# Sparse attention and token mixing on one core: first-pair edge units without decoding, first queries loaded earlier, half of the second pair's keys loaded later

## The chip, the core and the metric

The kernel runs on one NeuronCore of a Trainium2 chip. Its engines are named as in the profile: PE (TensorE) does matmuls, PEld is PE's weight load, DVE (VectorE) and ACT (ScalarE) do elementwise work and reductions, POOL (GpSimd) copies and issues indirect loads, and SP (SyncE) issues the other DMA transfers, one after the other, in program order. All transfers share 16 DMA engines. The metric is the device time of one execution in microseconds (us).

## The reference, cut to what matters

Block-sparse attention over 4 batches of 8 heads, 768 positions of 64 elements, in blocks of 32 (24 blocks). A query block attends to its neighbours, to the first and the last block, and to three sampled blocks; the first and the last query block attend to everything. The result, 512 wide, goes through token mixing.

```python
def _attn_ref(q, k, v, sampled_blocks):
    ...
    scores = scale * np.matmul(q, k.transpose(0, 1, 3, 2))
    ...
    mask = np.abs(blk_i - blk_j) <= window
    mask = mask | (blk_i == 0) | (blk_j == 0) | (blk_i == n_blocks - 1) | (blk_j == n_blocks - 1)
    for qb in range(n_blocks):
        for kb in sampled_blocks[qb]:
            mask[qb * block:(qb + 1) * block, kb * block:(kb + 1) * block] = True
    ...
    attn = attn / (np.sum(attn, axis=-1, keepdims=True) + 1e-09)
    return np.matmul(attn, v)

def _moe_ref(x, w_theta, w_tok_r, w_tok_i, w_ch):
    theta = x @ w_theta
    zr, zi = x * np.cos(theta), x * np.sin(theta)
    y = np.einsum('ts,bsd->btd', w_tok_r, zr) + np.einsum('ts,bsd->btd', w_tok_i, zi)
    u = x + y
    return u + np.maximum(u @ w_ch, 0.0)
```

## The kernel before

**Pairs and units.** The four batches are worked on as two pairs (`bp` 0 and 1). Each pair has 26 units: four wide or edge units, `WIDE`, which are the first and last query blocks for a quarter of the heads at a time (`b`, `pp`), against all keys; then 22 middle units, one for each query block from 1 to 22. So units 0 to 3 are the first pair's edge units, 4 to 25 its middle units, 26 to 29 and 30 to 51 those of the second pair.

**One unit.** PE computes scores (`S`, line 314; `SW`, line 407, for edge units), DVE takes a minimum of the negated scores (lines 316 and 413), ACT the exponential (lines 325 and 421), PE transposes the weights (`T` and `Tw`, line 331) into one PSUM tile, ACT copies that to `pT` (line 333), and PE multiplies with the values (`X`, line 365, once for two middle units; `Xw`, line 435). DVE divides by the sums (`xo`, line 350), and SP stores the result in DRAM (`xs`, lines 384 and 446).

**What a unit needs.** Middle units read keys that POOL gathers from the pair's key tile into `kg` (`gather_k`, line 275), since the sampled blocks are known only at run time; POOL then issues an indirect load of values, `vb` (line 297), and SP loads the neighbours' values, `va` (lines 293 and 294). Edge units read the key tile itself: it has eight groups, four for each `b`, and the unit (`b`, `pp`) reads groups 4b + pp·2 and the next. They read values that `load_v_wide` loads (780 KB each, line 397). Queries are loaded for two blocks at once (256 KB, line 236) and scaled by ACT (line 242).

**Keys.** The first pair's key tile lies in a room that later becomes weights and, before that, the second pair's values for edge units; the second pair's key tile `kb1` is a room of its own, loaded one group (384 KB) at a time, in eight loads (line 250), during units 5 to 19.

**Decoding.** The mixing weights arrive as 64-bit floats and are turned into a high and a low 32-bit part during attention, piece by piece. A piece has three phases: ACT takes the absolute value (line 69) and DVE rearranges bits (73 to 75); DVE scales the low word (81 and 83); ACT rounds to the high part (line 89) and DVE takes the rest (96 and 97). When a piece is done, SP loads the next but one (line 64). 20 pieces, 60 phases, are shared out over the units by weight: 1.5 for an edge unit, 1 for a middle unit, 0 for some. `decoder.ahead` issues ACT's part and `decoder.go` DVE's.

**Order.** The order is written out by hand in a loop over units `n`; each engine runs its instructions in that order. Loop `n` issues the scores of unit n + 1, the transposes and values of unit n (or of a pair of units before), and the gathers and scaling for unit n + 2. On ACT, `scale_q` of unit n + 2 comes first in a loop, ahead of unit n's `pT` copy, and `decoder.ahead` stands between the first `pT` copy of an edge unit and the next unit's exponential. Key and value loads for the second pair are SP instructions at the head of a loop; stores and `va` loads come at its end.

Of the kernel before, what the change touches and what calls it, by code (L numbers as in the profile page):

```python
# [193 lines left out]
def attention(tc, qT, qE, kT, vr, sampled, xs, ident, pieces, room, follow):  # L194
# [9 lines left out]
    with ExitStack() as ctx, ExitStack() as scored, ExitStack() as early:  # L204
# [27 lines left out]
        def load_q(bp, i):  # L232
            if i % 2 == 0:
                return
            t = qp.tile([P, 2, 2, 4, 32], F32, tag="q", name=f"q{bp}_{i}", bufs=Q_BUFS)
            nc.sync.dma_start(t.rearrange("r u b p f -> r u (b p f)"), qT[bp][:, i - 1 : i + 1, :])
            qbs[bp, i] = t
# [10 lines left out]
        def load_k(bp, g, n, s=slice(0, NB)):  # L248
            b = g // 4
            nc.sync.dma_start(kbs[bp][:, g : g + n, s], kT[bp, b][:, g - 4 * b : g - 4 * b + n, s])  # L250
# [5 lines left out]
        def load_edges(bp):  # L256
            qes[bp] = ep.tile([P, 2, 4, 64], F32, tag="qe", name=f"qe{bp}")
            nc.sync.dma_start(qes[bp].rearrange("r b p f -> r (b p f)"), qE[bp])

        def turn_edges(bp):  # L260
            t = qes[bp].rearrange("r b p f -> r (b p f)")
            nc.vector.tensor_scalar(t, t, -0.125, None, op0=ALU.mult)
# [125 lines left out]
        def load_v_wide(bp, b, pp):  # L388
            k = 2 * b + pp - 1
            if k < 0:  # L390
                v = vp.tile([P, 6, 260], F32, tag="vw", name=f"vw{bp}")
            else:
                if not k:
                    vrooms[bp] = room(("tok_r", "tok_i")[bp], f"vw{bp}").rearrange("p c f -> p (c f)")
                v = vrooms[bp][:, 1560 * k : 1560 * k + 1560].rearrange("p (c f) -> p c f", f=260)
            c0 = 260 * (2 * b + pp)
            nc.sync.dma_start(v, vr[768 * bp : 768 * bp + 768, c0 : c0 + 260].rearrange("(c s) f -> s c f", s=P))
            vws[bp, b, pp] = v
# [49 lines left out]
        WIDE = [(b, pp) for b in range(2) for pp in range(2)]  # L448
        units = []
# [1 line left out]
            units += [(bp, "w", x) for x in WIDE] + [(bp, i, None) for i in range(1, NB - 1)]  # L451
        shares, total = [], 0.0
        for n in range(len(units)):
            if n < 2 or n >= len(units) - 2 or units[n][1:] == ("w", WIDE[-1]):
                weight = 0.0
            else:
                weight = 1.5 if units[n][1] == "w" else 1.0
            total += weight
            shares.append(total)

        def do(n, inner, wide=None):

            if 0 <= n < len(units):
                bp, i, x = units[n]
                if i != "w":
                    inner(bp, i)
                elif wide:
                    wide(bp, *x)
# [4 lines left out]
        def first_of_pair(n):  # L473
            return n < len(units) and units[n][1] == "w" and units[n][2] == (0, 0)
# [3 lines left out]
        with tc.manual_schedule():  # L478
            load_edges(0)
            load_k(0, 0, 2, slice(0, 16))  # L480
            load_k(0, 0, 2, slice(16, NB))
            turn_edges(0)
            load_k(0, 2, 2)
            tab = Tables(nc, wp, sampled)
            load_v_wide(0, 0, 0)
            load_k(0, 4, 2)
            load_v_wide(0, 0, 1)
            load_k(0, 6, 2)
            load_v_wide(0, 1, 0)
            load_v_wide(0, 1, 1)  # L490
            for i in (1, 3):
                load_q(0, i)
            decoder = Decoder(pieces, stage, nc.sync)
            idle = ps_t.tile([P, 8, 128], F32, tag="T", name="idle")

            def turn_idle(n):
                for k in range(n):
                    nc.tensor.transpose(idle[:, k % 8, :], ident, ident)

            turn_idle(16)  # L500
            do(0, scores, scores_wide)
            turn_idle(10)
            tab.make(nc, cp)
            do(0, weights, weights_wide)
            for n in range(len(units) + 1):
                phases = 0
                if n < len(units):
                    phases = round(shares[n] / total * 3 * len(pieces)) - decoder.at
                if n + 5 < len(units) and not is_wide(n + 5) and units[n + 5][:2] not in ((0, 1), (0, 3)):
                    load_q(*units[n + 5][:2])  # L510
                if first_of_pair(n + 10):
                    load_edges(1)
                if first_of_pair(n + 12):
                    load_v_wide(1, 0, 0)
                for before, x in zip((2, 1, 0), WIDE[1:]):
                    if n and first_of_pair(n + before):
                        load_v_wide(1, *x)
                do(n + 2, gather_k)
                if n == len(units) - 16:
                    follow.send(vp)  # L520
                elif len(units) - 16 < n < len(units) - 4:
                    next(follow)
                elif n == len(units) - 3:
                    next(follow)
                if 5 <= n < 21 and n % 2:
                    load_k(1, (n - 5) // 2, 1)
                do(n + 3, number_blocks)
                do(n + 2, scale_q)
                if first_of_pair(n + 2):
                    turn_edges(1)  # L530
                if not is_wide(n):
                    decoder.ahead(phases)
                last = None
                if is_wide(n):
                    bp, _, x = units[n]
                    if n and not is_wide(n - 1):
                        last = units[n - 2][:2]
                        values(*last)
                        finish(*last)
                    turn_wide(bp, *x, 0)  # L540
                    decoder.ahead(phases)
                    do(n + 1, scores, scores_wide)
                    if n and is_wide(n - 1):
                        values_wide(bp, *units[n - 1][2], 1)
                    if is_wide(n + 1):
                        nx = units[n + 1]
                        weights_wide(nx[0], *nx[2], (0,))
                        turn_wide(bp, *x, 1)
                        weights_wide(nx[0], *nx[2], (1,))
                    else:  # L550
                        turn_wide(bp, *x, 1)
                        do(n + 1, weights, weights_wide)
                    values_wide(bp, *x, 0)
                    if n and is_wide(n - 1):
                        finish_wide(bp, *units[n - 1][2])
                    decoder.go(phases)
                    if n == 0:
                        tab.rest(nc)
                elif n == len(units):
                    last = units[n - 2][:2]  # L560
                    values(*last)
                    next(follow)
                    finish(*last)
                else:
                    bp, i, _ = units[n]
                    do(n + 1, scores, scores_wide)
                    if n == len(units) - 2:
                        early.close()
                        next(follow)
                    if i == 1:  # L570
                        values_wide(bp, *units[n - 1][2], 1)
                    elif i % 2:
                        last = bp, i - 2
                        values(*last)
                    if n == len(units) - 1:
                        scored.close()
                        next(follow)
                    if i % 2 and i > 1:
                        do(n + 1, weights, weights_wide)
                        if n == len(units) - 2:  # L580
                            next(follow)
                        turn(bp, i)
                    else:
                        turn(bp, i)
                        do(n + 1, weights, weights_wide)
                    decoder.go(phases)
                    if last:
                        finish(*last)
                    if n == len(units) - 1:
                        next(follow)  # L590
                    if i == 1:
                        finish_wide(bp, *units[n - 1][2])
                do(n + 2, load_pair)
                do(n + 2, gather_v)
            assert not decoder.left(), decoder.left()
            ctx.close()
            next(follow)
# [363 lines left out]
```

## Time and profile before

| | us |
|---|---|
| median of three runs | 586.22 |
| lowest and highest | 585.17, 587.04 |
| the profiled execution | 584.9 |
| its span, first to last instruction | 583.1 |
| PE busy in the span | 544.0 |
| DVE busy | 438.9 |
| ACT busy | 344.7 |
| POOL busy | 147.9 |

The profiled execution has 1.8 us around its span. Attention reaches from the start to about 233 us, where POOL ends, and token mixing from there to the end. The profile's timelines give, for one engine, start and length of each group of like instructions, its line in the kernel, the operation, what it writes and reads, and, in brackets, how long the engine stood idle before it and what released it. "issue" there means that the engine waited for nothing that the profile shows.

### The profile page before, as it was taken

To read this page: it belongs to the slowest core of one execution; us is meant where nothing else is said; L and a number is where in the kernel's file an instruction comes from. 1 tells how busy PE (TensorE), PEld (TensorE's weight loads), DVE (VectorE), ACT (ScalarE), POOL (GpSimd) and SP (SyncE) were. 2 spreads that over 40 slices of the span, in tenths; PEclk is the share of its full clock that TensorE was granted. 3 is DMA by queue.
4 is the path that set the end of the run, shared out by engine and by line. 5 is a ranking of instruction groups with operands and counts; after the bars stand their busy time and mean duration, and the time that the engine had idled before them with its cause. 6 is when DMAs were issued, how large, how long until landed. Compare 5 with 4: busy or idle time off the path is not lost.

```text
span 583.1 us, 16870 instructions
## 1 busy us (share of the span) xinstructions
PE 544.0 (93%) x6662; PEld 481.6 (83%) x6662; DVE 438.9 (75%) x1011; ACT 344.7 (59%) x734; POOL 147.9 (25%) x262
## 2 busy tenths in 40 slices
PE   7798888799989888999899999999999999999997
PEld 5465655566656666899899999999999999999997
DVE  4576888787889898879999896749848559547454
ACT  3685866767888777856766553456434456434510
POOL 1457768642589885000000000000000000000000
PEclk9998988999999989999999999999999999999999
DMA  8979899977699997545233333212421111212002
GB/s 293 351 216 323 260 364 349 300 241 271 200 299 291 317 296 227 156 123 151 85 100 101 105 115 98 65 44 61 136 84 63 57 48 46 78 55 72 6 1 108
DMA packets 64975, 95.60 MB, mean 164 GB/s; under 512 B 9216, under 2 KB 46976, under 8 KB 64896
## 3 DMA queue, kind: packets, MB, share of 16 engines
q1 hardware_dynamic: 58560, 71.09, 40.1%
q0 software_dynamic: 6336, 23.43, 12.1%
q8 instruction: 52, 0.85, 0.6%
q14 instruction: 27, 0.22, 0.1%
HBM read 81.90 MB, written 12.58 MB: 162 GB/s over the span
## 4 chain that ended last, share of the span: by engine, by line
PE 73%; DVE 8%; ACT 8%; issue 4%; SPq 3%; DMA 3%; ACTq 0%; DVEq 0%
PE y L721 10%; PE y L723 10%; PE y L722 10%; PE X L365 7%; PE T L331 6%; PE S L314 4%; PE o L744 4%; PE o L745 4%; PE o L746 4%; PE h L670 3%; PE h L669 3%; PE h L671 3%; ACT pT L333 3%; ACT P L325 2%; DMA q<-in_qT_dram 2%
## 5 line engine op out<-in xcount | busy, mean ns | idle before, releaser
L325 ACT ACTIVATE P<-S,m 128x256 f32<-128x256 f32 x176 | 69.3, 486 | 7.7 <-DVE m L316 7.3
L333 ACT COPY pT<-T 128x1024 f32<-128x1024 f32 x44 | 44.9, 1021 | 32.8 <-PE T L331 32.6
L316 DVE TENSOR_REDUCE m<-S 128x4 f32<-128x1024 f32 x44 | 53.6, 1218 | 13.8 <-PE S L314 13.5
L331 PE MATMUL T<-ident,P 128*128 128x128 f32 x352 | 51.7, 289 | 10.1 <-ACT pT L333 6.4
L331 PEld LDWEIGHTS T<-ident,P 128*128 128x128 f32 x352 | 39.9, 146 | 22.9 <-ACT pT L333 15.0
L676 ACT ACTIVATE t<-h,up_int 128x256 f32<-128x256 f32 x48 | 22.7, 475 | 58.6 <-PE h L671 55.6
L275 POOL COPY kg<-kb 128x256 f32 (+2 forms) x101 | 52.9, 564 | 17.1 <-PE S L314 17.0
L275 POOL COPY kg<-kb_tok_i 128x256 f32 (+2 forms) x101 | 48.4, 519 | 24.3 <-DMA kb_tok_i<-in_kT_dram 14.5
L297 POOL DMA_INDIRECT vb<-in_vr_dram,rows x44 | 44.6, 1013 | 38.8 <-PE X L365 33.6
L671 PE MATMUL h<-w_theta_hi,xTl 128*128 128x256 f32 x192 | 54.1, 282 | 0.2 <-DVE xTl L661 0.2
L669 PE MATMUL h<-w_theta_hi,xTh 128*128 128x256 f32 x192 | 54.1, 282 | 0.0
L314 PE MATMUL S<-kg,q 64*32 64x256 f32 x1408 | 51.5, 387 | 2.5 <-issue 2.4
L670 PE MATMUL h<-w_theta_lo,xTh 128*128 128x256 f32 x192 | 53.9, 281 | 0.0
L721 PE MATMUL y<-w_tok_r,zh 128*128 128x384 f32 x128 | 43.2, 337 | 0.8 <-ACT zh L701 0.8
L722 PE MATMUL y<-w_tok_i,zh 128*128 128x384 f32 x128 | 43.1, 337 | 0.0
L722 PE MATMUL y<-w_tok_r,zh 128*128 128x384 f32 x128 | 43.1, 336 | 0.0
L745 PE MATMUL o<-ul,w_ch_hi 128*128 128x384 f32 x128 | 42.9, 335 | 0.0
L746 PE MATMUL o<-uh,w_ch_lo 128*128 128x384 f32 x128 | 42.9, 335 | 0.0
L721 PE MATMUL y<-w_tok_i,zh 128*128 128x384 f32 x128 | 42.8, 337 | 0.0
L744 PE MATMUL o<-uh,w_ch_hi 128*128 128x384 f32 x128 | 42.4, 335 | 0.0
L723 PE MATMUL y<-w_tok_r,zl 128*128 128x384 f32 x128 | 42.4, 336 | 0.0
L686 ACT ACTIVATE cs<-rr 128x256 f32<-128x256 f32 x48 | 20.0, 416 | 37.9 <-DVE rr L681 37.6
(157 smaller groups left out, 1438.8 us busy)
## 6 DMA issues: line engine op xcount, KB each, us to landing
xa<-xs SPq DMA_DIRECT2D x192, 64.0 KB
out_dram<-of SPq DMA_DIRECT2D x32, 192.0 KB
va<-in_vr_dram SPq DMA_DIRECT2D x22, 260.0 KB
q<-in_qT_dram SPq DMA_DIRECT2D x22, 256.0 KB
xs<-xo SPq DMA_DIRECT2D x88, 64.0 KB
xr<-xs SPq DMA_DIRECT2D x84, 64.0 KB
raw_tok_r<-in_w_tok_r_dram SPq DMA_DIRECT2D x8, 512.0 KB
raw_tok_i<-in_w_tok_i_dram SPq DMA_DIRECT2D x8, 512.0 KB
```

The costliest lines, as they stand in the source:

```text
L275: nc.gpsimd.tensor_copy(dst, blocks.rearrange("r g s f -> r s g f"))
L314: nc.tensor.matmul(sc[32 * p : 32 * p + 32, e, b, :], q[rows, b, p, :], keys[rows, :, :, place(b, p), :], start=True, stop=True)
L325: nc.scalar.activation(pt[:, e, b, :], sc[:, e, b, :], AF.Exp, bias=m[:, e, b : b + 1], scale=-1.0)
L331: nc.tensor.transpose(t[:, k, :], pt, ident)
L669: nc.tensor.matmul(ps, hi[:, c, :], wh[:, c, :], start=c == 0, stop=False)
L670: nc.tensor.matmul(ps, hi[:, c, :], wl[:, c, :], start=False, stop=False)
L671: nc.tensor.matmul(ps, lo[:, c, :], wh[:, c, :], start=False, stop=c == 3)
L721: nc.tensor.matmul(acc, zh[:, dd], wh[j][:, tt], start=j == 0 and m == 0, stop=False)
L722: nc.tensor.matmul(acc, zh[:, dd], wl[j][:, tt], start=False, stop=False)
L723: nc.tensor.matmul(acc, zl[:, dd], wh[j][:, tt], start=False, stop=j == 5 and m == 1)
L745: nc.tensor.matmul(ps, wh[:, c, :], ul, start=False, stop=False)
L746: nc.tensor.matmul(ps, wl[:, c, :], uh, start=False, stop=c == 3)
```

## The change

Four edits to the written-out order; the bytes loaded are the same, in six key loads instead of eight.

1. Units 0 to 3 get no share of the decoding (before: units 0, 1 and 3 got none, unit 2 had weight 1.5). All later shares grow a little, as the 60 phases are now spread over a weight of 46.5 instead of 48.
2. The load of the first two query blocks goes to SP ahead of the last edge unit's value load instead of behind it.
3. The second pair's three later value loads for edge units each move one loop back: from loops 24, 25 and 26 to 25, 26 and 27.
4. Of the second pair's keys, groups 0 to 3 are loaded one at a time in loops 5, 9, 13 and 17, groups 4 and 5 together in loop 24, groups 6 and 7 together in loop 25 (before: one group in each odd loop from 5 to 19).

```diff
         for n in range(len(units)):
-            if n < 2 or n >= len(units) - 2 or units[n][1:] == ("w", WIDE[-1]):
+            if n < len(WIDE) or n >= len(units) - 2 or units[n][1:] == ("w", WIDE[-1]):
                 weight = 0.0
             else:
                 weight = 1.5 if units[n][1] == "w" else 1.0
...
             load_v_wide(0, 1, 0)
+            load_q(0, 1)
             load_v_wide(0, 1, 1)
-            for i in (1, 3):
-                load_q(0, i)
+            load_q(0, 3)
             decoder = Decoder(pieces, stage, nc.sync)
...
                 if first_of_pair(n + 12):
                     load_v_wide(1, 0, 0)
-                for before, x in zip((2, 1, 0), WIDE[1:]):
-                    if n and first_of_pair(n + before):
+                for before, x in zip((1, 0, -1), WIDE[1:]):
+                    if n > 1 and first_of_pair(n + before):
                         load_v_wide(1, *x)
                 do(n + 2, gather_k)
...
-                if 5 <= n < 21 and n % 2:
-                    load_k(1, (n - 5) // 2, 1)
+                if n in (5, 9, 13, 17):
+                    load_k(1, (n - 5) // 4, 1)
+                for before, g in ((2, 4), (1, 6)):
+                    if n and first_of_pair(n + before):
+                        load_k(1, g, 2)
                 do(n + 3, number_blocks)
```

## The prediction

> **What bounds the kernel now.** I read the page first for the span, then three stretches of the span side by side, then the timelines of the start, and last the PE timeline where the chain of waits says "issue".
>
> ```profile
> span 583.1 us, 16870 instructions
> ```
>
> ```profile
> 45.00:117.00 72.00, 59.50 (x1401) 42.70 (x1402) 57.79 (x85) 50.30 (x101) 52.85 (x90) 0.93 0.99 323
> 117.00:147.00 30.00, 27.69 (x522) 18.79 (x525) 24.20 (x42) 21.99 (x33) 9.09 (x15) 1.00 0.76 243
> 233.00:583.00 350.00, 342.88 (x2237) 340.29 (x2231) 254.53 (x702) 177.59 (x423) 0.00 (x0) 1.00 0.28 82
> ```
>
> The columns are the stretch and its length, then busy time (and instructions) of PE, PE's weight loads, DVE, ACT and POOL, the granted clock, the DMA share and GB/s. The last 350 us are token mixing, with PE busy for 342.88 of them: a microsecond saved ahead of 233 us comes out at the end as one. The change lies ahead of it, in attention. There no compute engine is full. From 45 to 117 us (middle units of the first pair) PE works 59.50 of 72 us, and the DMA engines are at a share of 0.99 with 323 GB/s: transfers are what is full, and half the change takes bytes out of this stretch. From 117 to 147 us (the second pair's edge units, where those bytes go) the share is 0.76.
>
> The start is read from the timelines of ACT, DVE, PE, POOL and SP.
>
> ```profile
> 23.79 0.63 ACT L242 ACTIVATE q<-q 128x512 f32<-128x512 f32 x1 [2.44 <-DMA q<-in_qT_dram]
> 24.32 0.78 ACT L333 COPY pT<-Tw 128x768 f32<-128x768 f32 x1
> 26.37 0.68 ACT L69 ACTIVATE da_theta<-raw_theta 128x512 f32<-128x512 f32 x1 [1.27 <-DMA raw_theta<-in_w_theta_dram]
> 26.95 0.90 ACT L421 ACTIVATE PW<-SW,mw 128x768 f32<-128x768 f32 x1
> 27.73 0.80 ACT L333 COPY pT<-Tw 128x768 f32<-128x768 f32 x1
> ...
> 23.04 1.82 DVE L413 TENSOR_REDUCE mw<-SW 128x1 f32<-128x768 f32 x2 [3.32 <-PE SW L407]
> ...
> 22.85 0.92 PE L435 MATMUL Xw<-vw_tok_r,pT 128*64 128x65 f32 x24
> 25.16 0.87 PE L331 MATMUL Tw<-ident,PW 128*128 128x128 f32 x6 [1.39 <-ACT pT L333]
> 28.59 0.87 PE L331 MATMUL Tw<-ident,PW 128*128 128x128 f32 x6 [1.71 <-ACT pT L333]
> ...
> 32.07 0.92 PE L435 MATMUL Xw<-vw_tok_r,pT 128*64 128x65 f32 x24
> ...
> 17.40 2.54 POOL L275 COPY kg<-kb_tok_i 128x512 f32<-128x512 f32 x6 [14.53 <-DMA kb_tok_i<-in_kT_dram]
> ...
> 6.54 5.31 SPq L397 DMA_DIRECT2D vw_tok_r<-in_vr_dram  x2
> ...
> 20.00:24.00 4.00, 3.52 (x58) 2.14 (x54) 0.96 (x2) 1.56 (x3) 3.72 (x7) 1.00 1.07 390
> ```
>
> ACT runs in program order, and two of its instructions here belong to nobody who is in a hurry. The scaling of the first queries (23.79) stands 2.44 us for its transfer, with edge unit 2's pT copy queued behind it; PE waits 1.39 us for that copy. The first decoding piece (da_theta, 26.37) stands 1.27 us for its words, with unit 3's exponential and the next pT copy behind it; PE waits 1.71 us.
>
> In the middle, PE stops inside a group of equal matmuls, with no engine to wait for:
>
> ```profile
> 110.39 0.55 PE L331 MATMUL T<-ident,P 128*128 128x128 f32 x3 [1.43 <-issue]
> 110.86 1.09 PE L314 MATMUL S<-kg,q 64*32 64x256 f32 x32
> 111.89 0.40 PE L372 MATMUL X<-first 1*128 1x260 bf16 x2
> 112.21 1.14 PE L365 MATMUL X<-vb,pT 128*32 128x65 f32 x64
> 113.28 1.03 PE L365 MATMUL X<-va,pT 128*64 128x65 f32 x26
> 115.92 0.45 PE L365 MATMUL X<-va,pT 128*64 128x65 f32 x6 [1.60 <-issue]
> ...
> 49.66 2.31 issue
> ...
> 114.30:116.30 2.00, 0.40 (x7) 0.31 (x7) 1.61 (x3) 1.75 (x5) 2.00 (x5) 1.00 0.76 234
> ...
> 52.00:54.00 2.00, 2.00 (x26) 1.88 (x26) 0.37 (x2) 0.00 (x0) 1.84 (x4) 0.50 1.05 277
> ```
>
> Between the two stops lie 3+32+2+64+26 = 127 matmuls, with their weight loads 254 instructions: the stops come at a fixed count of instructions, so PE is waiting for its instructions, and that in the stretch where the DMA engines are full. The chain of waits has six such stops above 0.4 us in the first pair's middle, from the one at 49.66 to the one that ends at 115.92; the first is followed by a stretch at a granted clock of 0.50.
>
> **The change, part by part.**
>
> *First queries sooner.* On SP's queue the two-block query load moves ahead of one 780 KB load of values. At the 390 GB/s of 20 to 24 us, 0.80 MB are 2.05 us, so the queries land at about 21.7 instead of 23.8. ACT has them scaled by 22.3 and the pT copy done by 23.0; PE then starts the next transposes when its own Xw ends, 22.85 + 0.92 = 23.77, not 25.16: 1.4 us sooner. The load moved behind (256 KB later, 0.7 us) is first read by the last edge unit's value matmuls at 32.07, so this costs nothing; without some 8 us of cover it would cost its 0.7.
>
> *No decoding in unit 2.* Alone, the queries' gain would die at da_theta, which waits for its words until 26.37 whatever comes before. With decoding gone from that unit (two phases), unit 3's first exponential waits only for its minimum, 23.04 + 0.92 = 23.96. It ends at 24.8, the copy behind it runs to 25.6, and PE's transposes of unit 3 start at 25.64 instead of 28.59. Both edits together: 2.95 us. The decoding edit alone, with the queries at 23.79, would give 1.7; the queries alone about nothing. What is late next is the scores of the first middle unit (29.39); POOL had gathered its keys by 17.40 + 2.54 = 19.9, so it follows.
>
> *The two phases done elsewhere.* The same 60 phases are spread over weights of 46.5 instead of 48: units 4 to 25 get 28 phases instead of 27, the second pair one more too. Two phases are this much work on DVE, and one ACT instruction of 0.68:
>
> ```profile
> 27.68:30.47 2.79, 2.65 (x6) 1.00 0.26 71
> ...
> 57.77 0.86 DVE da_theta L96
> ...
> 226.51 0.76 DVE raw_tok_i L83
> ```
>
> At most they cost 2.65 + 0.68 = 3.3 us, at least nothing, as DVE idles 14 of 72 us above. From 57.77 to 226.51 the chain holds 29 pieces of decoding, 17.2 us in all, for 58 phases: 0.30 us each. I take 0.6.
>
> *Half of the keys later.* Eight loads of one group (384 KB) in units 5 to 19 become four, in units 5, 9, 13 and 17, and two loads of two groups in units 24 and 25. From the first pair's middle 1.57 MB go. What bytes cost there is read from the two pairs, which run the same units, one with the key loads and one without; from the start of the first middle unit's scores to that of the last's (29.39 to 119.58, 146.94 to 229.69):
>
> ```profile
> 29.39 1.09 PE L314 MATMUL S<-kg,q 64*32 64x256 f32 x32
> ...
> 146.94 1.09 PE L314 MATMUL S<-kg,q 64*32 64x256 f32 x32
> ...
> 229.69 1.09 PE L314 MATMUL S<-kg,q 64*32 64x256 f32 x32
> ...
> 29.39:119.58 90.19, 76.81 (x1794) 54.39 (x1793) 72.72 (x109) 64.67 (x128) 63.63 (x109) 0.94 0.94 297
> 146.94:229.36 82.42, 73.40 (x1791) 51.90 (x1791) 71.94 (x113) 64.92 (x128) 66.97 (x109) 0.98 0.92 277
> ```
>
> The first pair takes 90.2 us, the second 82.8: 7.4 us more for 26.8 - 22.8 = 4.0 MB more, or 1.9 us per MB. For 1.57 MB that is 2.9 us. The upper end is a stretch wholly bound by transfers: 1.57 MB at 323 GB/s, 4.9 us. The lower end is -1: the other bytes may fill the room, and a stop that falls elsewhere may lengthen. I take 2.9, as it comes from like units.
>
> *The same bytes in the edge units.* These rows are from the timelines of SP, PE and POOL.
>
> ```profile
> 122.05 0.40 SPq L397 DMA_DIRECT2D vw_tok_i<-in_vr_dram  x1
> 128.30 1.05 SPq L397 DMA_DIRECT2D vw_tok_i<-in_vr_dram  x2
> ...
> 136.80 1.52 PE L407 MATMUL SW<-kb,qe 64*64 64x512 f32 x16
> 139.90 0.92 PE L435 MATMUL Xw<-vw_tok_i,pT 128*64 128x65 f32 x24
> 141.87 1.52 PE L407 MATMUL SW<-kb,qe 64*64 64x512 f32 x16
> ...
> 120.81 3.63 POOL L275 COPY kg<-kb 128x512 f32<-128x512 f32 x6 [2.76 <-PE S L314]
> ```
>
> The first two late groups take the place on SP of the value load at 122.05 and at 323 GB/s land at 124.5; PE reads them at 136.80. The last two go out at about 128.9 behind 0.80 MB of values and the queries, 1.85 MB in all: 134.6; PE reads them at 141.87. The value load moved to unit 25 is issued at 128.3 and read at 139.90, the last one goes out one unit, some 5 us (136.80 to 141.87), later than now and is read two units behind the one at 139.90. POOL, in order, now stands until 134.6 at its first gather of the second pair, where it ran at 120.81; behind it wait that gather (3.63), an indirect load of values and the next gather, and the first is read by the scores at 146.94. With 3.63 us of work it is done at 138.3, 8.6 us early. So no wait is added to the path; if that cover went, POOL's 3.63 us would lie on it.
>
> What is left is the fuller stretch: 243 GB/s over 30 us are 7.3 MB, and 1.57 more lift the share from 0.76 to about 0.92, that of the second pair. The edge units have no stop above 0.4 us now. The cost lies between -0.5 (a shift of stops) and 2.9 (as dear as where the bytes came from). I take 1.3, a little under the middle, since the new share is nearer to 0.99 than the old one but still below it.
>
> **Sum:** 2.95 + 2.9 - 0.6 - 1.3 = 3.95, about 3.9 us off. The profiled execution took 584.9 us for its span of 583.1, so 581.0; it stands 1.3 below the median of 586.2, so against the median **582.3 us**.
>
> **A rule beside the trace.** The row of 115.92 and the count of 127 show PE held up for its instructions. The Trainium skill, Runtime: NRT & Kernel Launch, section Instruction fetch mechanics, says that instructions are refilled in blocks of 256, with which the trace agrees (254 counted, weight loads included), and that the fetch is hidden, since an engine dispatches slower than blocks arrive; there the trace differs, with 1.43 and 1.60 us of waiting. By that rule taking bytes away would win nothing at these stops.
>
> **The rivals.**
>
> *The bytes move without effect.* The stops would be a matter of each fetch's own time and not of the load on the engines, so they stay as they are, and the edge units get none. For it: the stop of 1.60 us that ends at 115.92 falls where the share was 0.76 (114.30 to 116.30), so stops come without full engines too. Against it: 7.4 us between like pairs. Time: 586.2 - 2.95 + 0.6 = 583.9. This is what the rule above would make of it.
>
> *The change doesn't do what it says at the start.* The queries land no sooner, as transfers already in flight share the engines with them; then only the decoding edit works: 1.7 for 2.95, and with the bytes washing out, 2.9 won and 2.9 paid, 586.2 - 1.7 + 0.6 = 585.1, within 0.3% of before. For it: SP needs 5.31 us (from 6.54) to issue two value loads, so the queue is backed up already. Against: it is backed up with just the load that the queries pass.
>
> *The edge units become the bound (slower).* They hold 522 matmuls, 522 / 127 = four of PE's blocks. If the two loads fill the engines there as in the middle, each block could stop PE as at 49.66: 2.31 us, and 1.0 more for the 2 us at half clock. Three such stops are 9.9 us: 586.2 - 2.95 - 2.9 + 0.6 + 9.9 = 590.9. It decides from 5.25 us on, between one such stop and two. For it: three value loads and the keys, 4.0 MB, are issued within some 15 us. Against: the share averages 0.92, and in these units PE's next work waits for ACT and DVE anyway.
>
> **How the numbers follow.** Forecast case 0.50 (its own range 579.5 to 584.3, the relief from 1 to 4.9 and the edge cost from 0 to 2.9); bytes without effect 0.20; start half done 0.17; edge units the bound 0.13. A measurement of this kernel tells about 0.3%, 1.8 us, from no change. The forecast and the first rival lie beyond that, though each with a tail inside: faster 0.66, same 0.20, slower 0.14. For the range, the low end takes full relief, a free edge stage and the whole start, 586.2 - 2.95 - 4.9 + 0.6 = 578.9, less 0.9 for the runs' own scatter: 578.0. The high end takes in the second rival and the beginning of the third: 587.5.
>
> **What would show it.** Right: ACT's first q scaling at about 22 us, no da_theta before the first middle unit's exponential, the third unit's Tw near 25.6 and the first middle scores near 26.4; from there to the last middle scores of the first pair 87 to 88 us instead of 90.2, with fewer or shorter "issue" stops; SW of the last edge units not waiting for kb; the share from 117 to 147 near 0.92 and that stage at most 2 us longer. Wrong: q still landing at 23.8; 90 us again between the middle scores; new "issue" stops or a clock of 0.5 in the edge units; the scores after the edge units waiting for POOL; DVE's decoding longer on the chain than 17.2 us.

## The result, and the profile after

The changed kernel takes 0.9946 of the time of before (95% interval 0.9922 to 0.9971); the medians of 20 runs each are 581.34 and 582.66 us. At 582.66 us the ratio is 3.1 us (1.7 to 4.5). The ratio is of the fast runs alone and leaves out five of the changed kernel's twenty runs, each over 1.5% above its fastest; over all runs the means differ by 2.0 us and the medians by 1.3. Forecast were 3.9. On another chip, beside the last experiments below, the same kernel gave 0.9892 (0.9839 to 0.9945).

The profiled execution has a span of 577.6 us against 583.1. That is 5.5 us, more than the ratio says, since single executions of one kernel differ by several microseconds; the stages are read from it, the size from the ratio. Marks of its stages, us from the span's start, and the lengths between them:

| | before | after | difference of the length |
|---|---|---|---|
| start to first middle scores | 29.39 | 26.15 | -3.24 |
| to the first pair's last middle scores | 119.58 | 112.86 | 90.19 to 86.71, -3.48 |
| to the second pair's first middle scores | 146.94 | 140.70 | 27.36 to 27.84, +0.48 |
| to the last unit's minimum on DVE | 230.89 | 226.07 | 83.95 to 85.37, +1.42 |
| to the end | 583.1 | 577.6 | 352.21 to 351.53, -0.68 |

ACT's timeline of the start, after the change:

```profile
21.29 0.63 ACT L242 ACTIVATE q<-q 128x512 f32<-128x512 f32 x1 [0.33 <-DMA q<-in_qT_dram]
21.82 0.78 ACT L333 COPY pT<-Tw 128x768 f32<-128x768 f32 x1
23.70 0.90 ACT L421 ACTIVATE PW<-SW,mw 128x768 f32<-128x768 f32 x1 [1.09 <-DVE mw L413]
24.50 0.79 ACT L333 COPY pT<-Tw 128x768 f32<-128x768 f32 x1
```

and PE's, with the marks of the table:

```profile
21.01 1.52 PE L407 MATMUL SW<-kb_tok_i,qe 64*64 64x512 f32 x16
...
25.34 0.88 PE L331 MATMUL Tw<-ident,PW 128*128 128x128 f32 x6 [0.31 <-ACT pT L333]
26.15 1.09 PE L314 MATMUL S<-kg,q 64*32 64x256 f32 x32
...
112.86 1.09 PE L314 MATMUL S<-kg,q 64*32 64x256 f32 x32
...
130.43 1.52 PE L407 MATMUL SW<-kb,qe 64*64 64x512 f32 x16
135.50 1.52 PE L407 MATMUL SW<-kb,qe 64*64 64x512 f32 x16
...
140.70 1.09 PE L314 MATMUL S<-kg,q 64*32 64x256 f32 x32
```

The wait for the queries is 0.33 us, no decoding stands ahead of the exponential at 23.70, which waits for its minimum alone, and PE's two waits of 1.39 and 1.71 us have become one of 0.31. The edge units' scores that read the late groups (130.43 and 135.50) have no wait for them.

The stages by windows, columns as in the prediction; the first row is the edge stage of the kernel before, the others are of the changed kernel:

```profile
119.58:146.94 27.36, 25.18 (x471) 17.22 (x471) 21.67 (x37) 20.46 (x31) 8.13 (x14) 1.00 0.79 258
```

```profile
26.15:112.86 86.71, 75.26 (x1794) 52.65 (x1793) 69.11 (x109) 64.91 (x128) 66.39 (x110) 0.96 0.92 294
112.86:140.70 27.84, 25.37 (x471) 17.22 (x470) 23.03 (x38) 20.96 (x32) 9.45 (x15) 1.00 0.90 301
```

In the first pair's middle the share of the DMA engines went from 0.94 to 0.92 and the granted clock from 0.94 to 0.96; in the edge stage the share rose from 0.79 to 0.90, and the stage is half a microsecond longer.

POOL in the edge stage of the changed kernel:

```profile
129.77 3.51 POOL L275 COPY kg<-kb 128x512 f32<-128x512 f32 x6 [16.69 <-issue]
133.43 0.97 POOL L297 DMA_INDIRECT vb<-in_vr_dram,rows  x1
```

and SP's last key load:

```profile
122.07 0.54 SPq L250 DMA_DIRECT2D kb<-in_kT_dram  x1
```

POOL stood 16.69 us. The profile names no releaser; that it stood for the last key groups is inferred from the load at 122.07. It was done with the first gather at 133.3, 7.4 us ahead of the scores that read it.

### The profile page after: what moved, and what is told of

The parts are those of the page before. It is cut to its first block, busy times and chain, and to the rows that moved or that the text cites. A ratio compares the mean times of both kernels' runs of the same rounds, so it can differ in the third digit from the quotient of the medians.

```text
span 577.6 us, 16874 instructions
## 1 busy us (share of the span) xinstructions
PE 541.1 (94%) x6662; PEld 478.8 (83%) x6662; DVE 435.6 (75%) x1011; ACT 344.5 (60%) x734; POOL 153.1 (26%) x262
## 4 chain that ended last, share of the span: by engine, by line
PE 73%; DVE 10%; ACT 8%; issue 4%; DMA 2%; SPq 1%; ACTq 0%; DVEq 0%
PE y L724 12%; PE y L726 11%; PE y L725 11%; PE X L365 5%; PE T L331 5%; PE S L314 4%; PE o L747 4%; PE o L749 4%; PE o L748 4%; PE h L673 4%; PE h L674 4%; PE h L672 4%; ACT P L325 3%; ACT pT L333 3%; DVE m L316 3%
## 5 line engine op out<-in xcount | busy, mean ns | idle before, releaser
L275 POOL COPY kg<-kb_tok_i 128x256 f32 (+2 forms) x101 | 51.5, 549 | 19.4 <-DMA vw_tok_r<-in_vr_dram 15.7
L297 POOL DMA_INDIRECT vb<-in_vr_dram,rows x44 | 46.5, 1058 | 29.8 <-PE X L365 24.5
```

The lines of the kernel that those rows point to most:

```text
L275: nc.gpsimd.tensor_copy(dst, blocks.rearrange("r g s f -> r s g f"))
```

## The experiments

All were timed in five rounds beside the kernel before on the same chip; a ratio is to that.

**1 to 3: the start taken apart.** First the decoding edit alone, then the query load alone, then both.

```diff
-            if n < 2 or n >= len(units) - 2 or ...
+            if n < len(WIDE) or n >= len(units) - 2 or ...
```

> Only the decoding edit: units 0 to 3 decode nothing, all loads as before. Theory of the prediction (one chain at the start: first queries, then da_theta): the first queries still land at 23.8 us, the third edge unit's second pT copy no longer stands behind da_theta, and the first middle unit's scores start about 1.7 us sooner than the 29.4 of before. Rival (the queries alone set the start): they start at 29.4 as before. The two phases done later cost 0.6; in time about 1 us faster, within scatter.

```diff
+            load_q(0, 1)
             load_v_wide(0, 1, 1)
-            for i in (1, 3):
-                load_q(0, i)
+            load_q(0, 3)
```

> Only the first query load moved ahead of the last value load. Theory of the prediction: the queries land near 21.5 us, but ACT then stands at da_theta until its words land at 26.3, so the first middle unit's scores start at 29.4 us, less at most 0.3: no gain. Rival (the queries alone set the start): scores at about 27.9, 1.4 us sooner. Time: same.

> Both start edits, keys and later value loads as before. Theory of the prediction: first middle scores at about 26.2 to 26.4 us, 3 us sooner, and the 3 us stay: the last middle unit's scores of the first pair come 2.5 to 3 us sooner, time 2.3 us (0.4%) less than before. Rival (the middle of the first pair is bound by transfers): the 3 us are eaten on the way, the stretch between first and last middle scores grows from 90.2 to 92 or more, and the time is the same as before.

Measured: 0.9985 (0.9951 to 1.0018) with the decoding edit, 1.0014 (0.9978 to 1.0051) with the query load, 0.9954 (0.9920 to 0.9988) with both. Neither alone can be told from no change; both together are 2.7 us faster. That the 3 us are eaten in the first pair's middle is out: 88.24 us there, not 92. The profiled execution with both, at 585.07 us, was one of the longer ones (median 582.89); it lost 4.3 us against the kernel before in the second pair's middle, so its span shows no gain.

How the two share it was predicted too finely. PE's timeline from unit 3's edge scores to the first middle scores; the first of them in the kernel before, whose middle scores at 29.39 stand in the prediction:

```profile
21.40 1.52 PE L407 MATMUL SW<-kb_tok_i,qe 64*64 64x512 f32 x16
```

decoding edit alone:

```profile
23.98 1.52 PE L407 MATMUL SW<-kb_tok_i,qe 64*64 64x512 f32 x16
...
29.17 1.09 PE L314 MATMUL S<-kg,q 64*32 64x256 f32 x32
```

query load alone, and ACT's wait in it:

```profile
22.55 1.52 PE L407 MATMUL SW<-kb_tok_i,qe 64*64 64x512 f32 x16
...
28.49 1.09 PE L314 MATMUL S<-kg,q 64*32 64x256 f32 x32
```

```profile
25.48 0.68 ACT L69 ACTIVATE da_theta<-raw_theta 128x512 f32<-128x512 f32 x1 [1.77 <-DMA raw_theta<-in_w_theta_dram]
```

both:

```profile
21.94 1.52 PE L407 MATMUL SW<-kb_tok_i,qe 64*64 64x512 f32 x16
...
27.08 1.09 PE L314 MATMUL S<-kg,q 64*32 64x256 f32 x32
```

From these edge scores to the first middle scores the kernel before needs 29.39 - 21.40 = 7.99 us, the decoding edit alone 5.19, the query load alone 5.94, both 5.14, the changed kernel 5.14. But the edge scores themselves start anywhere from 21.0 to 24.0 us. In the execution with the decoding edit alone they came 2.6 us late. PE's rows ahead of them:

```profile
16.47 1.21 PE L331 MATMUL Tw<-ident,PW 128*128 128x128 f32 x6 [2.36 <-ACT pT L333]
17.61 2.81 PE L407 MATMUL SW<-kb_tok_i,qe 64*64 64x512 f32 x16
```

DVE works on the sampled blocks' numbers ahead of the second edge unit's minimum; here it waits 0.60 us for their transfer and starts at 10.55 us, not 9.62. PE then stood 2.36 us (1.66 before), and its next scores took 2.81 us for 1.52, at a granted clock of 0.57 from 16.47 to 20.40 us, against 1.00 from 15.50 to 17.80 in the kernel before. Behind that the queries weren't late any more. With the query load alone ACT did stand at da_theta, as expected (1.77 us), but its words came at 25.5 instead of 26.4. One execution each can't part the two edits to a microsecond. The timed ratios speak for both being needed, but their intervals overlap, so that isn't shown.

Over more executions the start is clearer. With both edits the first middle scores come 5.1 us behind those edge scores in each of seven, at 26.15 to 27.82 us. With the start as before (the kernel before, experiment 4 and the second doubling of 5) they come 7.99, 7.14 and 6.14 us behind, at 29.39, 28.56 and 28.88. The mean gain is 1.9 us; the pair of executions in the table of stages is at the upper end. The first doubling of 5 (6.13 us, at 28.88) is not in the mean, and the kernel with zeros is not because its start is held up: DVE's scaling of the edge queries (line 262), 0.43 us in the kernel before, takes 4.87 beside POOL's 5.22 us of writing zeros.

**4: the later loads alone.** The start and the decoding are those of before; the diff is the last part of the change.

> Only the loads of the second pair's keys and edge values as in the changed kernel; start and decoding as before. Theory of the prediction (bytes cost 1.9 us per MB in the full stretch): from first to last middle scores 2.9 us less than 90.2, edge stage 0.5 to 1.3 us more than 27.4; time 1.6 to 2.4 us less. Rival (stops of PE have nothing to do with the bytes): 90.2 as before, and the time the same.

0.9963 (0.9927 to 0.9999), 2.2 us faster. In its profiled execution the middle takes 88.83 us and the edge stage 26.82: 1.4 us less in the middle, half of what was expected, and nothing paid back. But 88.83 also lies within what the middle takes with all keys loaded there (87.5 to 90.2 in four executions), so this one execution doesn't show the gain.

**5: no key loads at all, and twice the key loads.** To size the bytes' price, doses beyond the change's own. Without any, the second pair's keys are zeros written by POOL at the start:

```diff
             tab.make(nc, cp)
+            nc.gpsimd.memset(kbs[1], 0.0)
...
-                if 5 <= n < 21 and n % 2:
-                    load_k(1, (n - 5) // 2, 1)
```

> The kernel before, without any load of the second pair's keys: POOL writes zeros into their tile at the start, so that the second pair's attention is on zero keys; everything else as before. 3.15 MB less. Theory (1.9 us per MB): first to last middle scores 90.2 - 6.0 = 84 us, near the second pair's 82.8; edge stage 27 us as before; time 1% less. Rival (bytes without effect; the pairs differ for another reason): 90 us, time the same.

With each group loaded twice, in successive loops:

```diff
-                if 5 <= n < 21 and n % 2:
+                if 5 <= n < 21:
                     load_k(1, (n - 5) // 2, 1)
```

> The kernel before, with each of the eight key groups of the second pair loaded twice, in each of units 5 to 20 one load: 3.15 MB more in the first pair's middle, nothing else. Theory (bytes cost 1.9 us per MB there, by way of PE's waits for instructions): first to last middle scores 90.2 + 6.0 = 96 us, more and longer issue stops; time 1% more than before. If the stretch is wholly bound by transfers: 9.7 us, 100. Rival (bytes without effect): 90 us, same time.

and three loops apart:

```diff
                 if 5 <= n < 21 and n % 2:
                     load_k(1, (n - 5) // 2, 1)
+                if 8 <= n < 24 and n % 2 == 0:
+                    load_k(1, (n - 8) // 2, 1)
```

> The kernel before with each of the eight key groups loaded a second time, now three loops behind its first load (loops 8 to 22) instead of in the next loop, so that SP needn't stand for the first copy to land. 3.15 MB more. Theory (bytes cost 1.7 to 1.9 us per MB in the full stretch): first to last middle scores 90.2 + 5.5 to 6 = 96 us, time 1% more. If the stretch is bound by transfers outright (323 GB/s): 100 us, 1.7% more. Rival (bytes without effect): 90 us. If it is again near 110, the transfers and not SP's wait made the earlier doubling so dear.

The first pair's middle, without key loads:

```profile
29.71:113.23 83.52, 73.93 (x1793) 51.57 (x1792) 70.20 (x110) 64.55 (x128) 66.78 (x109) 0.98 0.92 280
```

and with two loads of each group, three loops apart:

```profile
28.88:123.45 94.57, 76.88 (x1793) 53.17 (x1792) 70.61 (x110) 65.21 (x128) 63.53 (x109) 0.95 0.99 321
```

83.5, 90.2 and 94.6 us for 0, 3.15 and 6.29 MB: 2.1 and 1.4 us per MB, 1.8 over both. The times go the same way: 0.9922 (0.9886 to 0.9958) without, 4.6 us less, and 1.0056 (1.0019 to 1.0094) with twice, 3.3 us more. So the loads have an effect, the price taken from the two pairs (1.9) was about right, and a stretch bound by transfers outright (3.1 us per MB) is not what this is. That it is the bytes, and not the number of loads that SP issues, is not tested.

The doubling in successive loops failed as a measure of bytes: 1.0295 (1.0213 to 1.0378), on three runs. SP's waits in its profiled execution, of 606.0 us:

```profile
SPq L250 <- DMA kb<-in_kT_dram: 33.5, 8, 7.4
```

The second load of a group waits on SP until the first has landed, 33.5 us in eight waits, and everything behind it on SP waits too. Three loops apart that was 8.2 us, and the price fell to 3.3 us; so the upper dose isn't wholly free of SP's waits either.

Whether the bytes act by way of PE's waits for instructions is seen where the same stop can be found in several kernels. PE's timeline with each group loaded twice, and the windows around the stop:

```profile
113.87 1.03 PE L365 MATMUL X<-va,pT 128*64 128x65 f32 x26 [0.17 <-DMA va<-in_vr_dram]
118.46 0.66 PE L365 MATMUL X<-va,pT 128*64 128x65 f32 x6 [3.56 <-issue]
```

```profile
114.90:118.50 3.60, 0.04 (x3) 0.04 (x2) 1.35 (x3) 2.63 (x6) 2.43 (x6) 1.00 1.05 303
118.50:121.00 2.50, 2.50 (x22) 2.05 (x27) 2.36 (x6) 0.01 (x1) 0.00 (x0) 0.51 1.03 403
```

It comes after 26 of 32 matmuls, as the stop of 1.60 us in the kernel before; here it is 3.56 us and half clock follows. The stop after the ninth of 32, in the kernel before:

```profile
49.15 0.51 PE L365 MATMUL X<-va,pT 128*64 128x65 f32 x9
51.97 1.57 PE L365 MATMUL X<-va,pT 128*64 128x65 f32 x23 [2.31 <-issue]
```

in the changed kernel:

```profile
46.71 0.92 PE L365 MATMUL X<-va,pT 128*64 128x65 f32 x23 [0.42 <-issue]
```

without key loads:

```profile
51.36 0.92 PE L365 MATMUL X<-va,pT 128*64 128x65 f32 x23 [0.91 <-issue]
```

but with the later loads alone:

```profile
51.64 1.16 PE L365 MATMUL X<-va,pT 128*64 128x65 f32 x23 [2.58 <-issue]
```

So the places are fixed by the instruction count and the lengths are not. The DMA view of the first pair's middle, in the kernel before, has a row that fits:

```profile
q8 instruction: 14, 0.23, 1.1%
```

These are 14 packets of some 16 KB; PE runs 1794 matmuls and 1793 weight loads there, about 256 to a packet. With six stops above 0.4 us on the chain, most packets pass without one.

The stops above 0.4 us on the chain through this stretch add to 7.3 us without key loads, 8.2 before and 13.3 with twice, a part of the 11 us between the ends. But they add to 8.5 us in the changed kernel, and to 14.7 with the two start edits of experiment 3, whose key loads are those of before and whose middle took 88.24 us. So the effect of the loads is shown, its way through these stops is not: with the same key loads, experiment 3 has 6.5 us more of them than the kernel before, and a middle 2.0 us shorter.

**6: three quarters late.** Groups 2 and 3 in loop 22, so that six of eight groups are loaded just ahead of the edge units (loops 22, 24 and 25).

```diff
-                if n in (5, 9, 13, 17):
-                    load_k(1, (n - 5) // 4, 1)
-                for before, g in ((2, 4), (1, 6)):
+                if n in (5, 13):
+                    load_k(1, (n - 5) // 8, 1)
+                for before, g in ((4, 2), (2, 4), (1, 6)):
```

> The changed kernel with groups 2 and 3 late too (two groups in each of units 22, 24 and 25; groups 0 and 1 in units 5 and 13). Theory (1.9 us per MB in the middle, next to nothing in the edge units): 0.79 MB less between the middle scores, 1.5 us, of which unit 22 gives some back: 0.5 to 1.5 us faster than the changed kernel, about 0.993 of before. Rival (the edge units are full by now): edge stage above 29 us, the time 0.9946 of before or more.

0.9941 (0.9904 to 0.9977). Middle 83.48 us, edge stage 27.88 at a share of 0.95: the edge units bear this too. In time it can't be told from the changed kernel.

**7: where the displaced phases cost.** After the first runs it looked as if the decoding edit cost 2 us at the end of attention: from the last scores to the first mixing matmul 14.5 us without it, 16.5 with it in the changed kernel, since unit 48 now has two phases on DVE. Two remedies: to stop decoding two units sooner, or to have the first pair's middle take both phases.

```diff
-            if n < len(WIDE) or n >= len(units) - 2 or ...
+            if n < len(WIDE) or n >= len(units) - 4 or ...
```

> The changed kernel, with no decoding in the last four units instead of the last two, so that it is finished two units sooner. Theory (the respread phases cost at one place, the last units, where DVE is the bound: from the last scores to the first token-mixing matmul 14.5 us without the decoding edit, 16.5 to 17.9 with it): that stretch returns to 14.5 us or less, and the kernel is about 2 us faster than the changed one, 0.987 to 0.991 of before. Rival (two phases cost their share wherever they stand): the second pair's middle grows by the same 2 us, from 82.2 to 84, and the time is that of the changed kernel, 0.9946.

```diff
-                weight = 1.5 if units[n][1] == "w" else 1.0
+                weight = 1.5 if units[n][1] == "w" else 1.0 if units[n][0] else 23.5 / 22
```

> The changed kernel, with the first pair's middle units weighted 23.5/22, so that they take both displaced phases and units 26 to 49 decode just as before the change. Theory (the respread phases cost 2 us at the last units only): last scores to first token-mixing matmul 14.5 us instead of 16.5; first pair's middle at most 0.6 us more; time 1.5 to 2 us less than the changed kernel run beside it. Rival (two phases cost 2 us wherever DVE does them): the first pair's middle 1.5 to 2 us longer, time that of the changed kernel.

The stretch did return to 14.57 and 14.53 us, and the times did not follow: 0.9976 (0.9941 to 1.0011) and 0.9963 (0.9919 to 1.0008), the second beside 0.9892 for the changed kernel. The mark was badly chosen. DVE's last minimum and PE's first mixing matmul, before:

```profile
230.89 1.23 DVE L316 TENSOR_REDUCE m<-S 128x4 f32<-128x1024 f32 x1
```

```profile
244.21 0.41 PE L721 MATMUL y<-w_tok_r_hi,zh 128*128 128x384 f32 x1 [0.34 <-DVE xo L350]
```

after:

```profile
222.87 1.09 PE L314 MATMUL S<-kg,q 64*32 64x256 f32 x32
...
226.07 1.22 DVE L316 TENSOR_REDUCE m<-S 128x4 f32<-128x1024 f32 x1
```

```profile
239.38 0.41 PE L724 MATMUL y<-w_tok_r_hi,zh 128*128 128x384 f32 x1 [0.34 <-DVE xo L350]
```

13.3 us in both. In the changed kernel PE issues the last scores earlier (222.87) and they wait longer for DVE, 3.2 us for the 1.2 from 229.69 to 230.89; the 2 us were PE's lead and no loss. In three other executions with the decoding edit (alone, with both start edits, and with three quarters late) this stretch is 14.8 us, but from the last minimum to the end they take 352.5 to 353.0 us, against 352.2 before and 351.5 in the changed kernel. A loss of 2 us there is out; one of some tenths is not.

**8: both variants together, and the changed kernel again.**

> Both together: keys of groups 2 to 7 late, and the displaced phases in the first pair's middle. Theory: 14.5 us from the last scores to token mixing, middle of the first pair 84 to 86 us, edge stage 28: 2.5 to 3.5 us less than the changed kernel beside it, about 0.988 of before. Rival (gains don't add): no less than the changed kernel.

> The changed kernel itself, on the same chip and beside the same runs of before as the two variants of it. Theory: 0.9946 of before again, 0.992 to 0.997; middle of the first pair 86 to 88 us, last scores to token mixing 16.5 to 17.9.

0.9883 (0.9828 to 0.9939) and 0.9892 (0.9839 to 0.9945), 580.35 and 578.41 us in the median of six runs: no difference. No variant beats the changed kernel by more than the runs scatter. In its second profiled execution the changed kernel starts the middle at 26.53 us and takes 85.37, 27.82 and, to the last minimum, 84.35 us.

Put side by side by the bytes of the second pair's keys loaded in the first pair's middle, the profiled executions (without the doubling in successive loops) give, in us:

| MB | executions | first pair's middle | edge stage | stops above 0.4 us on the middle's chain |
|---|---|---|---|---|
| 0 | 1 | 83.5 | 28.8 | 7.3 |
| 0.79 | 2 | 83.5 and 86.5, mean 85.0 | 27.9, 28.0 | 7.1, 1.6 |
| 1.57 | 5 | 85.4 to 88.8, mean 86.8 | 26.8 to 28.9, mean 27.9 | 6.3 to 10.4 |
| 3.15 | 4 | 87.5 to 90.2, mean 88.8 | 26.7 to 27.9, mean 27.3 | 7.1 to 14.7 |
| 6.29 | 1 | 94.6 | 26.8 | 13.3 |

Some of these kernels differ in the start and the decoding too. A straight line through the thirteen rises by 1.7 us per MB; the stops don't follow the bytes.

## Why the prediction was right

*The start, 2.95 us.* 3.24 by the two profiled executions, 2.85 from the edge scores on; both edits by themselves 2.7 us in time, and 1.9 as the mean over the executions compared behind experiments 1 to 3. The queries' landing (21.7 forecast, 21.3 seen), the exponential at 23.96 (23.70) and the third unit's Tw at 25.64 (25.34) came as worked out. The waits named are gone, so the mechanism held; the size was taken from an execution in which they were long. The split between the two edits (1.7 and nothing) was not confirmed.

*The bytes out of the middle, 2.9 us.* 3.5 and 4.8 in two executions of the changed kernel against one of before, 1.4 with the later loads alone, 2.0 between the means for 1.57 and 3.15 MB; 1.7 us per MB over all doses, so 2.6 for 1.57 MB. The price from the two pairs held. The mechanism named for it, fewer and shorter stops, was not confirmed: the stops' sum is no smaller in the changed kernel (8.5 us for 8.2), and 14.7 in a kernel with the key loads of before. By which wait the loads act stays open.

*The edge stage, 1.3 us.* +0.48 and +0.46 in the changed kernel, less than nothing with the later loads alone, 0.6 between the means. The term was over-sized: at a share of 0.90, against the 0.92 forecast, these units have no stop above 0.4 us in the changed kernel. (The prediction calls 1.3 a little under the middle of its bounds of -0.5 and 2.9; the middle is 1.2.) The covers named for the keys and for POOL's gather held, the latter with 7.4 us for 8.6.

*The displaced phases, 0.6 us.* Not shown. The second pair to its last minimum took 1.4 and 0.4 us more in the two executions of the changed kernel, but that stretch runs from 82.6 to 88.3 us over the executions, and with the phases moved to the first pair it was no shorter (87.4 and 86.5).

*The rivals.* Loads without effect: out by the doses. A start half done: out by the queries at 21.29. Edge units as the bound: out by 27.84. The rule of the Trainium skill, Runtime: NRT & Kernel Launch, section Instruction fetch mechanics, that fetching is hidden, is not what these runs show, if the stops are what their fixed places suggest: one of 3.56 us came with the DMA engines at 1.05.

The sum of the terms, 3.9 us, stands against 3.1 (1.7 to 4.5) measured. Part of that is luck: by the means, both gains were taken too large, and so was the cost of the edge stage against them. The forecast case's own range, 579.5 to 584.3, is narrower than its bounds give (578.9 to 585.8). The forecast time, 582.3, was a difference from a median of three runs, 586.2; twenty runs put that median at 582.66, so part of the agreement of the bare times, 581.34, is luck too.

## What to carry to other kernels

An instruction that waits for a transfer on an in-order engine charges its wait to all that is queued behind it: look for two such instructions in a row, since mending one of them may show nothing in time, as here (0.9985 and 1.0014). Where transfers are nearly full, price bytes by two like stretches of the same trace that differ in bytes, check the price over several executions, and move the bytes to a stretch whose share leaves room. Before a stretch is called slower, check that both its marks lie on the path.

## What the runs showed that I had not expected

Executions of one kernel differ a good deal, and the granted clock goes with it: of the changed kernel's runs, one at a mean clock of 0.998 took 577.56 us and one at 0.985 took 583.67. The fourth edge unit's scores start at 21.0 us in one execution and at 24.0 in another, mostly by a transfer of the sampled blocks' numbers that came late and a clock of 0.57 behind PE's wait. A difference of one or two microseconds in a stage of one profiled execution is therefore no evidence by itself.
